# Ten heads instead of eight transposed on TensorE, and their normalisation shared between ScalarE and POOL

## The chip, the cores and the metric

One core of a Trainium2 chip runs one program. The time is device microseconds of one execution; beside it stands a profiled execution of the same kernel. The engines are called PE (TensorE; PEld is its weight load), DVE (VectorE), ACT (ScalarE), POOL (GpSimd) and SP (SyncE, which here only starts DMAs).

## What is computed

Attention over four batches of eight heads, 768 positions of 64 columns, in which a query sees only the keys with its own hash bucket (six signs of a random projection); then, for each of the 3072 positions, a two-layer network with a squared ReLU. The weights come as 64-bit floats, so the kernel has to decode them.

```
q_bits = (einsum('bhsd,dk->bhsk', q, proj) > 0)          # 6 bits, the same for k
mask   = q_bucket[:, :, :, None] == k_bucket[:, :, None, :]
scores = scale * matmul(q, k.transpose(0, 1, 3, 2))
scores = where(mask, scores, -1e9);  scores -= max(scores, -1)
attn   = exp(scores);  attn = attn / (sum(attn, -1) + 1e-9)
x      = matmul(attn, v)                                  # then (tokens, 512)
h = x @ w_in;  r = maximum(h, 0.0);  g = s * (r * r) + b
out = g @ w_out
```

## The kernel before

The program is a list of steps (`Plan.add`, `Plan.any`), each with an engine, a cost, what it reads and writes, and a priority (lower goes first). `Plan.order` runs a list scheduler over these numbers once, while the program is built: at each point an engine that is free takes the ready step with the lowest priority. A step with several ways (`any`) goes to the engine on which it would end first. What comes out is a fixed order on every engine, and on the chip each engine works through its order, waiting at each instruction for what it needs. So a change of a cost or a priority moves instructions everywhere behind it.

**Slots.** The attention is cut into 96 slots: 4 batches x 8 heads x 3 groups of 256 queries. A slot has two tiles of 128 queries by 768 keys. Per tile PE computes the masked scores into two PSUM banks (L568, L569; the mask is part of the product), DVE takes the row maximum (L573), ACT the exponential with its row sum (L574). Small steps on POOL (L578, L579) and DVE (L584, L585) form the reciprocal of the sum, and `norm` (L594, on POOL) multiplies the tile by it and adds the value that a row without any key gets.

**Two ways to the second product.** Its left operand is the tile transposed. In the first `FULL` heads (early) PE transposes the f32 tile, 12 transposes a slot in three steps (L621), ACT or DVE copies each step out of PSUM (L199 to `tb`), and PE multiplies it with the values (L628). In the later heads (`late(w)`) ACT writes the f16 high part (L598), DVE the low part (L599), SP starts a DMA transpose of each tile (L600), and PE multiplies with f16 values (L635).

**Before each head** PE transposes its queries and keys (L438) and computes the hash (L455 to L457), DVE makes the mask rows from it (L459), and DMAs copy them into place (`aq<-aq`, `ks<-nat`, `bq<-nat`) before the head's first score. These pieces get the priority `pr + PP` and are placed between the steps of the slots before (`between`, L636).

**Weights.** 32 blocks of 512 KB come in on ACT's DMA queue (L339) and are decoded on ACT, DVE and POOL (L343 to L354 and L356 to L387); `decodes` (L746) asks for 0.8 blocks a slot from the fourth slot on, and for six a slot from slot 21. For w_out the last step is the low part, high part subtracted from the value (L354); for w_in high and low part are scaled (L381, L386) by a power of two that needs the maximum over all partitions, which `spread` gets by a PE transpose of a broadcast column into PSUM (L394).

**The network.** When all eight heads of a batch have a group of 256 positions (xsb, written at L662 to L666 and passed through DRAM), `moe` takes it: eight rounds of a first product (L702 to L704), a chain on ACT and POOL (L712 to L716) and a second product (L727 to L729). Its steps have a priority behind those of the attention and fill PE where that leaves room; batch 0 can start at slot 21, and what is left after slot 95 runs alone.

Of the kernel before, what the change touches and what calls it, by code (L numbers as in the profile page):

```python
# [139 lines left out]
def lsh_attention_moe(ctx: ExitStack, tc, q, k, v, proj, w_in, w_out, s, b, out):  # L140
# [26 lines left out]
    def f32(ap):  # L167
        return ap.bitcast(F32)
# [8 lines left out]
    def pe(cost, fn, r, w, pr):  # L177
        plan.add(PE, cost, fn, r, w, pr)
# [7 lines left out]
    def pool(n, fn, r, w, pr, ns=None):  # L186
        plan.add(POOL, (0.15 + n / 430.0 if ns is None else ns), fn, r, w, pr)
# [135 lines left out]
    def decode(u, pr):  # L323
# [24 lines left out]
        if not wi:  # L348
            def swap():
                wt[key] = wk.tile([P, 2, 512], F32R, tag=f"w{u}", name=f"w{u}")  # L350
            pool(512, lambda: nc.gpsimd.tensor_tensor(gi, gi, raw()[:, :, 0], ALU.add), rk, [gk], pr)
            plan.add(None, 0.0, swap, [], rk + wk_, pr)
            copy(512, lambda: wt[key][:, 0], lambda: g, [gk], [key + (0,)], pr, (ACT, POOL))
            pool(512, lambda: nc.gpsimd.tensor_tensor(wt[key][:, 1], g, f32(wt[key][:, 0]), ALU.subtract), [gk, key + (0,)], [key + (1,)], pr)  # L354
            return
        pool(512, lambda: nc.gpsimd.tensor_tensor(raw()[:, :, 0], gi, raw()[:, :, 0], ALU.add), [gk], rk, pr)  # L356
        held_raw.append((raw, rk, key))
# [15 lines left out]
        for raw_, rk_, key_ in held_raw:  # L373
            def split(raw_=raw_, rk_=rk_, key_=key_):
                def swap():
                    wt[key_] = wk.tile([P, 2, 512], F16, tag=f"wi{key_[1]}_{key_[2]}", name=f"wi{key_[1]}_{key_[2]}")

                def src_():
                    return raw_()[:, :, 0].bitcast(F32)
                plan.add(None, 0.0, swap, [], [key_ + (0,), key_ + (1,)], pr)  # L380
                some(512, lambda e: e.activation(wt[key_][:, 0], src_(), AF.Copy, scale=up) if e is nc.scalar else e.tensor_scalar(wt[key_][:, 0], src_(), up, None, ALU.mult), rk_ + [("wsc", n)], [key_ + (0,)], pr, (ACT, POOL))  # L381

                def rest():
                    nc.gpsimd.tensor_scalar(src_(), src_(), up, None, ALU.mult)
                    nc.gpsimd.tensor_tensor(wt[key_][:, 1], src_(), wt[key_][:, 0], ALU.subtract)
                plan.any([(DVE, 0.75, lambda: nc.vector.scalar_tensor_tensor(wt[key_][:, 1], src_(), up, wt[key_][:, 0], ALU.mult, ALU.subtract)),  # L386
                          (POOL, 1.95, rest)], [("wsc", n), key_ + (0,)], rk_ + [key_ + (1,)], pr)  # L387
            split()
        held_raw.clear()

    def spread(m, mk_, pr):


        pe(0.12, lambda: nc.tensor.transpose(out=bank[:, 4, CH:CH + P], in_=m.broadcast_to([P, P]), identity=ident), [mk_], ["all"], pr)  # L394
        return bank[:, 4, CH:CH + P], "all"

    def inverse_power(up, down):

# [154 lines left out]
    def weights(i, pr):  # L553

        bb, h, c, w = slots[i]
        x, y = w % 2, i % NST
        aq, bq, ks = AQ[x], BQ[x], KS[x]
        nm, z, rz, u, big_ = [st[:, y, m] for m in range(5)]
        nk, zk = [[("st", y, m, a) for a in range(TPC)] for m in range(2)]
        for a in range(TPC):  # L560
            t, j = c * TPC + a, TPC * i + a
            b0 = (6 if i < EARLY else TWO if late(w) else 0) if j % 2 else 0
            bk = [("b", b0), ("b", b0 + 1)]
            ts = slice(t * P, (t + 1) * P)
            for g in range(2):
                def mm(g=g, ts=ts, b0=b0):
                    cols, o = slice(g * HS, (g + 1) * HS), bank[:, b0 + g, 0:HS]
                    nc.tensor.matmul(o, aq[:, ts], ks[0][:, cols], start=True, stop=False)  # L568
                    nc.tensor.matmul(o, bq[0:HR, ts], ks[1][0:HR, cols], start=False, stop=True)  # L569
                pe(mmc(HS, 2), mm, AK(x) + KK(x) + BK(x), [bk[g]], pr)  # L570
            e, ek = EB[ering(j)], EK[ering(j)]
            sc = bank[:, b0:b0 + 2, 0:HS]
            dve(S, lambda a=a, sc=sc: nc.vector.tensor_reduce(nm[:, a:a + 1], sc, AX.XY, ALU.max, negate=True), bk, [nk[a]], pr, 0.95)  # L573
            act(S, lambda a=a, sc=sc, e=e: nc.scalar.activation(e.rearrange("p (g n) -> p g n", g=2), sc, AF.Exp, bias=nm[:, a:a + 1], accum_out=z[:, a:a + 1]),  # L574
                bk + [nk[a]], [ek, zk[a]], pr, 0.28)

        def missing():
            nc.gpsimd.tensor_scalar(big_, nm, -FLOOR, 1e30, ALU.is_gt, ALU.mult)  # L578
            nc.gpsimd.tensor_scalar(u, nm, -FLOOR, 1.0 / (S + EPS), ALU.is_gt, ALU.mult)  # L579
        pool(TPC, missing, nk, [("st", y, 3), ("st", y, 4)], pr, 0.5)  # L580

        def inverse():
            for a in range(TPC):
                nc.vector.tensor_scalar(rz[:, a:a + 1], z[:, a:a + 1], EPS, big_[:, a:a + 1], ALU.add, ALU.add)  # L584
            nc.vector.reciprocal(rz, rz)  # L585
        dve(1, inverse, zk + [("st", y, 4)], [("st", y, 2)], pr, 0.5)
        for a in range(TPC):
            j = TPC * i + a
            e, ek = EB[ering(j)], EK[ering(j)]
            n, r = j % 2, i % 2  # L590
            hi, lo, hk = pb[:, n, 0], pb[:, n, 1], EK[NE + n]

            def norm(eng, a=a, e=e):
                eng.tensor_scalar(e, e, rz[:, a:a + 1], u[:, a:a + 1], ALU.mult, ALU.add)  # L594
            pool(S, lambda norm=norm: norm(nc.gpsimd), [("st", y, 2), ("st", y, 3)], [ek], pr, NORM if late(w) else 1.02)
            if not late(w):
                continue
            act(S, lambda e=e, hi=hi: nc.scalar.mul(hi, e, TOP), [ek], [hk], pr)  # L598
            dve(S, lambda e=e, hi=hi, lo=lo: nc.vector.scalar_tensor_tensor(lo, e, TOP, hi, ALU.mult, ALU.subtract), [ek, hk], [("lo", n)], pr, 1.0)  # L599
            plan.add(SP, TCOST, lambda a=a, n=n, r=r: nc.sync.dma_start_transpose(tb[:, r, a].rearrange("p h t q -> p (h t) q"), pb[:, n].rearrange("p h n -> p (h n)")),  # L600
                     [hk, ("lo", n)], TK(r, a, 2), pr, TLAG)
# [4 lines left out]
    def values(i, pr, pieces):  # L606
# [48 lines left out]
        if hh:  # L655
# [7 lines left out]
                pool(CH, lambda: nc.gpsimd.tensor_tensor(xsb[:, 1, :], t, xsb[:, 0, :], ALU.subtract), xk + [("xs", 0)], [("xs", 1)], pr)  # L663
            else:
                some(CH, lambda e: e.activation(xsb[:, 0, :], t, AF.Copy, scale=up) if e is nc.scalar else e.tensor_scalar(xsb[:, 0, :], t, up, None, ALU.mult), xk + [("sc", bb)], [("xs", 0)], pr, (ACT, POOL))
                dve(CH, lambda: nc.vector.scalar_tensor_tensor(xsb[:, 1, :], t, up, xsb[:, 0, :], ALU.mult, ALU.subtract), xk + [("sc", bb), ("xs", 0)], [("xs", 1)], pr, 0.45)  # L666
            xd[key] = tc.dram_tile([P, 2, CH], F16, name=f"xd{key[0]}_{key[1]}_{key[2]}")
            plan.add(SP, 0.7, lambda: nc.sync.dma_start(xd[key], xsb), [("xs", 0), ("xs", 1)], [("xd", key)], pr, 131072 / RATE_DMA)

# [135 lines left out]
QDUP = "pool"  # L805
RATE_DMA = 2.2e5
GATE = lambda KK, AK: AK(0)
FULL = 8
FPC = 0.62
WP = -8  # L810
MP = 0.0
PP = -5


# [24 lines left out]
```

## Time and profile before

| | us |
|---|---|
| median of 3 runs (range) | 1024.14 (1021.83 to 1026.34) |
| the profiled execution, and its span in the profile | 1022.31, 1020.5 |
| PE busy | 935.1 (92%) |
| DVE, ACT, POOL busy | 654.9 (64%), 644.9 (63%), 636.2 (62%) |

The span is what the instructions cover; the 1.8 us beside it lie before and after them. The profiled execution is 1.8 us below the median. A busy share is an average over stages that differ: the first 24 slots with nothing but attention and decoding, the stretch in which the network begins, a long middle with both, and the end with the network alone. Waits are put down to what released them last.

### The profile page before, as it was taken

The page shows a single profiled execution, that of the slowest core. Times are in us where ns is not written, and L with a number is a line of the kernel's source. Part 1 is how long each engine was busy: PE and PEld are TensorE (multiplying, and loading weights), DVE is VectorE, ACT ScalarE, POOL GpSimd, SP SyncE. Part 2 cuts the span into 40 slices and gives each one's busy share as a digit, 9 for nine tenths or more (in the row PEclk, how much of TensorE's full clock was granted, in tenths as well). Part 3 has the DMA queues.
Part 4 walks back from the last instruction along what each step waited for, and adds up shares of the span by engine and source line. Part 5 has one row for each costly group of instructions (what it writes and reads, how often), then busy time and mean ns, then how long its engine had stood idle before and what let it go on. Part 6 is the DMA issues. An engine that isn't in the chain of part 4 may idle for free.

```text
span 1020.5 us, 17422 instructions
## 1 busy us (share of the span) xinstructions
PE 935.1 (92%) x6080; PEld 742.6 (73%) x6080; DVE 654.9 (64%) x1189; ACT 644.9 (63%) x1165; POOL 636.2 (62%) x707
## 2 busy tenths in 40 slices
PE   6879787788489999999999999999999999999998
PEld 5656455566267887777888887787888888888886
DVE  6878788789687887877887777876678841000000
ACT  3667677776477676677767776776776764434442
POOL 2455756879497766766667776767766864333333
PEclk7999789889699999999999999999999999999999
DMA  3376475567949897898798989989798862101000
GB/s 100 103 197 182 103 193 145 161 190 154 176 94 179 159 195 169 165 194 186 164 188 187 174 174 195 168 168 200 146 181 187 153 129 63 42 1 42 12 22 21
DMA packets 319080, 144.41 MB, mean 142 GB/s; under 512 B 282688, under 2 KB 303680, under 8 KB 318992
## 3 DMA queue, kind: packets, MB, share of 16 engines
q1 hardware_dynamic: 313792, 126.25, 59.5%
q10 hardware_dynamic: 5200, 17.05, 5.8%
q8 instruction: 48, 0.79, 0.3%
q14 instruction: 40, 0.33, 0.1%
HBM read 48.24 MB, written 12.58 MB: 60 GB/s over the span
## 4 chain that ended last, share of the span: by engine, by line
PE 39%; issue 12%; POOL 10%; DVE 5%; DMA 3%; ACT 2%; SPq 0%; POOLq 0%; DVEq 0%; ACTq 0%
PE bank L635 7%; POOL glb L716 4%; PE bank L729 4%; PE bank L727 4%; PE bank L728 4%; PE bank L702 4%; PE bank L568 4%; PE bank L704 4%; PE bank L703 4%; PE bank L569 3%; POOL rb L715 3%; DVE pb L599 2%; DMA tb<-pb 2%; DVE st L573 1%; PE bank L438 1%
## 5 line engine op out<-in xcount | busy, mean ns | idle before, releaser
L594 POOL TENSOR_SCALAR eb<-eb,st 128x768 f32<-128x768 f32 x179 | 213.4, 1197 | 69.9 <-DVE st L585 66.7
L702 PE MATMUL bank<-xc,wi 128*128 128x256 f16 x768 | 211.7, 276 | 5.9 <-POOL wi L381 2.6
L573 DVE TENSOR_REDUCE st<-bank 128x1 f32<-128x768 f32 x192 | 181.1, 953 | 56.1 <-PE bank L569 45.2
L703 PE MATMUL bank<-xc,wi 128*128 128x256 f16 x768 | 209.8, 273 | 1.4 <-DVE wi L386 1.4
L704 PE MATMUL bank<-xc,wi 128*128 128x256 f16 x768 | 209.9, 273 | 0.0
L574 ACT ACTIVATE eb<-bank,st 128x768 f32<-128x768 f32 x179 | 160.2, 895 | 65.3 <-DVE st L573 53.9
L599 DVE SCALAR_TENSOR_TENSOR pb<-eb,pb 128x768 f16<-128x768 f32 x144 | 161.4, 1124 | 48.0 <-ACT pb L598 47.4
L568 PE MATMUL bank<-ks,aq 128*128 128x384 f32 x384 | 151.1, 393 | 26.1 <-ACT eb L574 14.1
L715 POOL TENSOR_SCALAR rb<-rb,misc 128x512 f32<-128x512 f32 x96 | 84.5, 881 | 141.2 <-ACT ghb L714 140.8
L727 PE MATMUL bank<-w,ghb 128*128 128x512 f32 x384 | 160.4, 418 | 0.0
L729 PE MATMUL bank<-w,glb 128*128 128x512 f32 x384 | 153.5, 400 | 7.4 <-POOL glb L716 7.2
L728 PE MATMUL bank<-w,ghb 128*128 128x512 f32 x384 | 151.9, 396 | 0.4 <-POOL w L354 0.4
L598 ACT ACTIVATE pb<-eb 128x768 f16<-128x768 f32 x144 | 120.1, 836 | 36.7 <-DMA tb<-pb 26.8
L569 PE MATMUL bank<-ks,bq 76*128 76x384 f32 x384 | 135.5, 353 | 5.6 <-DMA bq<-nat 3.7
L716 POOL TENSOR_TENSOR glb<-rb,ghb 128x512 fp32r<-128x512 f32 x96 | 131.1, 1366 | 5.5
L712 ACT ACTIVATE rb<-bank,dsc 128x512 f32<-128x512 f32 x74 | 50.9, 688 | 125.5 <-PE bank L704 115.9
L635 PE MATMUL bank<-tb,vb 128*128 128x256 f16 x864 | 108.2, 276 | 12.4 <-DMA tb<-pb 11.7
L568 PEld LDWEIGHTS bank<-ks,aq 128*128 128x128 f32 x384 | 76.2, 198 | 49.4 <-ACT eb L574 20.7
L702 PEld LDWEIGHTS <-wi 128*128 128x128 f16 x768 | 75.1, 98 | 44.3 <-issue 34.6
L740 DVE COPY osb<-bank 128x256 f32<-128x256 f32 x4 | 1.5, 420 | 163.3 <-PE bank L729 162.7
L635 PEld LDWEIGHTS <-vb 128*128 128x128 f16 x864 | 81.5, 99 | 34.0 <-issue 23.1
L578 POOL TENSOR_SCALAR st<-st 128x2 f32<-128x2 f32 x96 | 40.4, 421 | 90.7 <-DVE st L573 81.7
(128 smaller groups left out, 1656.9 us busy)
## 6 DMA issues: line engine op xcount, KB each, us to landing
ks<-aq SPq DMA_DIRECT2D x60, 192.0 KB
raw<-in_moe_w_in_dram ACTq DMA_DIRECT2D x16, 512.0 KB
raw<-in_moe_w_out_dram ACTq DMA_DIRECT2D x16, 512.0 KB
nat<-in_q_dram SPq DMA_DIRECT2D x32, 192.0 KB
nat<-in_k_dram SPq DMA_DIRECT2D x32, 192.0 KB
vm<-in_v_dram SPq DMA_DIRECT2D x32, 192.0 KB
xd<-xsb SPq DMA_DIRECT2D x48, 128.0 KB
xc<-xd SPq DMA_DIRECT2D x48, 128.0 KB
```

Source lines behind the costliest of these rows:

```text
L568: nc.tensor.matmul(o, aq[:, ts], ks[0][:, cols], start=True, stop=False)
L573: dve(S, lambda a=a, sc=sc: nc.vector.tensor_reduce(nm[:, a:a + 1], sc, AX.XY, ALU.max, negate=True), bk, [nk[a]], pr, 0.95)
L594: eng.tensor_scalar(e, e, rz[:, a:a + 1], u[:, a:a + 1], ALU.mult, ALU.add)
L599: dve(S, lambda e=e, hi=hi, lo=lo: nc.vector.scalar_tensor_tensor(lo, e, TOP, hi, ALU.mult, ALU.subtract), [ek, hk], [("lo", n)], pr, 1.0)
L635: nc.tensor.matmul(av, VB[x][:, kt].rearrange("p z d -> p (z d)"), t[:, :, h, kt], start=(h == kt == 0), stop=(h == 1 and kt == NT - 1))
L702: nc.tensor.matmul(hp, w[:, 0, fs], xc[:, 0, :], start=(cc == 0), stop=False)
L703: nc.tensor.matmul(hp, w[:, 1, fs], xc[:, 0, :], start=False, stop=False)
L704: nc.tensor.matmul(hp, w[:, 0, fs], xc[:, 1, :], start=False, stop=(cc == NC_ - 1))
L716: pool(2 * CH, lambda r=r, gh=gh, gl=gl: nc.gpsimd.tensor_tensor(gl, r, f32(gh), ALU.subtract), [rk, hk], [lk], MP)
L727: nc.tensor.matmul(o, gh[:, ts], w[:, 0], start=(f == 0), stop=False)
L728: nc.tensor.matmul(o, gh[:, ts], w[:, 1], start=False, stop=False)
L729: nc.tensor.matmul(o, gl[:, ts], w[:, 0], start=False, stop=(f == NF - 1))
```

## The change

Five things are edited; the line numbers of the changed program are up to nine higher.

- `FULL` goes from 8 to 10: the heads 8 and 9, the slots 24 to 29, take the early way, with transposes on PE.
- The normalisation of an early tile may go to POOL (cost `NORM`, 1.1, where it was 1.02) or to ACT (0.87), as the scheduler finds.
- In decoding, the low part of a w_out block may go to DVE (0.85) besides POOL (1.4); the cost of w_in's low part on DVE is 0.9 where it was 0.75. The low part of an early result (xsb) may go to POOL as two instructions (1.3) besides DVE (0.6, was 0.45).
- `spread` writes into unused columns of bank 0, one of the score banks, where it wrote into those of bank 4, the bank of the second product.
- `PP` goes from -5 to 0: the pieces that prepare the next heads get a later priority.

```
-            pool(512, lambda: nc.gpsimd.tensor_tensor(wt[key][:, 1], g, f32(wt[key][:, 0]), ALU.subtract), [gk, key + (0,)], [key + (1,)], pr)
+            plan.any([(POOL, 1.4, lambda: nc.gpsimd.tensor_tensor(wt[key][:, 1], g, f32(wt[key][:, 0]), ALU.subtract)),
+                      (DVE, 0.85, lambda: nc.vector.tensor_tensor(wt[key][:, 1], g, f32(wt[key][:, 0]), ALU.subtract))], [gk, key + (0,)], [key + (1,)], pr)
...
-                plan.any([(DVE, 0.75, lambda: nc.vector.scalar_tensor_tensor(wt[key_][:, 1], src_(), up, wt[key_][:, 0], ALU.mult, ALU.subtract)),
+                plan.any([(DVE, 0.9, lambda: nc.vector.scalar_tensor_tensor(wt[key_][:, 1], src_(), up, wt[key_][:, 0], ALU.mult, ALU.subtract)),
...
-        pe(0.12, lambda: nc.tensor.transpose(out=bank[:, 4, CH:CH + P], in_=m.broadcast_to([P, P]), identity=ident), [mk_], ["all"], pr)
-        return bank[:, 4, CH:CH + P], "all"
+        pe(0.12, lambda: nc.tensor.transpose(out=bank[:, 0, HS:HS + P], in_=m.broadcast_to([P, P]), identity=ident), [mk_], ["all"], pr)
+        return bank[:, 0, HS:HS + P], "all"
...
-            pool(S, lambda norm=norm: norm(nc.gpsimd), [("st", y, 2), ("st", y, 3)], [ek], pr, NORM if late(w) else 1.02)
+            ways = [(POOL, NORM, lambda norm=norm: norm(nc.gpsimd))]
+            if not late(w):
+                ways.append((ACT, 0.87, lambda a=a, e=e: nc.scalar.activation(e, e, AF.Identity, bias=u[:, a:a + 1], scale=rz[:, a:a + 1])))
+            plan.any(ways, [("st", y, 2), ("st", y, 3)], [ek], pr)
...
-                dve(CH, lambda: nc.vector.scalar_tensor_tensor(xsb[:, 1, :], t, up, xsb[:, 0, :], ALU.mult, ALU.subtract), xk + [("sc", bb), ("xs", 0)], [("xs", 1)], pr, 0.45)
+
+                def rest():
+                    nc.gpsimd.tensor_scalar(t, t, up, None, ALU.mult)
+                    nc.gpsimd.tensor_tensor(xsb[:, 1, :], t, xsb[:, 0, :], ALU.subtract)
+                plan.any([(DVE, 0.6, lambda: nc.vector.scalar_tensor_tensor(xsb[:, 1, :], t, up, xsb[:, 0, :], ALU.mult, ALU.subtract)), (POOL, 1.3, rest)],
+                         [("sc", bb), ("xs", 0)], xk + [("xs", 1)], pr)
...
-FULL = 8
+FULL = 10
...
-PP = -5
+PP = 0
```

Of the 60 normalisations of the ten early heads ACT gets 35 and POOL 25; of the 44 of the first 22 slots, 24 and 20. Of the 16 low parts of w_out DVE gets 10 and POOL 6; three low parts of w_in and three of xsb go to POOL as two instructions each. The order on ACT near the start, from the third exponential on, before:

```order
L574 ACTIVATE eb,st<-bank,st 128x768 x3
L539 ACTIVATE vm,vmx<-vm 128x384
L574 ACTIVATE eb,st<-bank,st 128x768
L199 COPY tb<-bank 128x512
L574 ACTIVATE eb,st<-bank,st 128x768
L653 ACTIVATE xpb<-bank 64x256
L199 COPY tb<-bank 128x512
L574 ACTIVATE pb,st<-bank,st 128x768
L539 ACTIVATE vm,vmx<-vm 128x384
```

And of the changed program at the same place (L575 is now the exponential, L598 the normalisation, L657 the result's copy):

```order
L575 ACTIVATE eb,st<-bank,st 128x768 x3
L598 ACTIVATE eb<-eb,st 128x768
L575 ACTIVATE eb,st<-bank,st 128x768
L199 COPY tb<-bank 128x512 x2
L575 ACTIVATE eb,st<-bank,st 128x768
L598 ACTIVATE eb<-eb,st 128x768
L657 ACTIVATE xpb<-bank 64x256
L575 ACTIVATE pb,st<-bank,st 128x768
L199 COPY tb<-bank 128x512 x2
L598 ACTIVATE eb<-eb,st 128x768
```

About every second exponential is now followed by a normalisation, which waits for a reciprocal of DVE, and the next exponential stands behind it.

The order on SP while the heads 8 and 9 are computed, before (L600 is the DMA transpose of a tile, L175 and L415 are copies and loads for the next heads, L527 loads values):

```order
L600 DMA_TRANSPOSE tb<-pb 128x12x128 x2
L175 DMA ks_70<-aq_66 64x768
L600 DMA_TRANSPOSE tb<-pb 128x12x128
L175 DMA ks_70<-aq_66 64x768
L175 DMA ks_70<-bq_68 64x768
L600 DMA_TRANSPOSE tb<-pb 128x12x128
L175 DMA aq_66<-aq_66 64x768
L175 DMA ks_70<-nat_65 12x768
L175 DMA bq_68<-nat_65 12x768
L600 DMA_TRANSPOSE tb<-pb 128x12x128 x2
```

And of the changed program (L538 loads values for their maximum, L697 loads the network's input):

```order
L175 DMA ks_70<-aq_66 64x768 x2
L538 DMA vm<-in_v_dram 128x384
L175 DMA ks_70<-bq_68 64x768
L528 DMA vn<-in_v_dram 128x384
L538 DMA vm<-in_v_dram 128x384 x2
L175 DMA aq_66<-aq_66 64x768
L697 DMA xc_1_1_2465<-xd_2_1_147 128x512
L697 DMA xc_1_1_2465<-xd_3_1_150 128x512
L175 DMA ks_70<-nat_65 12x768
L175 DMA bq_68<-nat_65 12x768
```

No transpose stands here any more; the first comes with head 10, some 20 rows further on. On ACT's queue the last weight block is asked for at the exponentials of slot 29 before and of slot 28 now, so before the first transposes of head 10.

On PE, from the last hash product of head 2 to its first score (`ks_70`), before:

```order
L457 MATMUL bank<-bq_68,pj_118 64x384
L628 MATMUL bank<-tb,vb_80 64x256 x6
L568 MATMUL bank<-ks_71,aq_67 128x384
L569 MATMUL bank<-ks_71,bq_69 128x384
L568 MATMUL bank<-ks_71,aq_67 128x384
L569 MATMUL bank<-ks_71,bq_69 128x384
L621 MATMUL bank<-ident,eb 128x128 x12
L568 MATMUL bank<-ks_70,aq_66 128x384
```

And of the changed program, where four more scores of head 1 and four transposes stand between the hash and these rows (L632 is the second product, L625 the transpose):

```order
L632 MATMUL bank<-tb,vb_80 64x256 x6
L395 MATMUL bank<-ident,vmx 128x128
L569 MATMUL bank<-ks_71,aq_67 128x384
L570 MATMUL bank<-ks_71,bq_69 128x384
L569 MATMUL bank<-ks_71,aq_67 128x384
L570 MATMUL bank<-ks_71,bq_69 128x384
L625 MATMUL bank<-ident,eb 128x128 x12
L632 MATMUL bank<-tb,vb_80 64x256 x6
L569 MATMUL bank<-ks_70,aq_66 128x384
```

More of PE's work now stands between this hash and the score that needs it.

## Rows read from the trace of the kernel before

**Rows 1.** Stages: start:end length, busy us (instructions) per engine, clock, DMA share, GB/s

```profile
12.00:174.50 162.50, 130.97 (x770) 91.95 (x770) 131.59 (x281) 109.14 (x232) 88.05 (x112) 0.89 0.55 145
174.50:330.00 155.50, 122.80 (x732) 91.98 (x731) 124.45 (x229) 103.28 (x190) 121.09 (x112) 0.89 0.71 160
330.00:830.00 500.00, 487.93 (x3317) 400.74 (x3316) 382.38 (x632) 350.94 (x626) 351.31 (x402) 1.00 0.87 174
830.00:1020.50 190.50, 185.39 (x1231) 151.82 (x1228) 8.71 (x16) 78.82 (x115) 73.10 (x73) 1.00 0.14 38
```

**Rows 2.** The same view around the first late heads

```profile
214.00:256.80 42.80, 36.14 (x200) 27.57 (x199) 37.70 (x66) 28.33 (x50) 37.36 (x31) 0.92 0.70 159
256.80:277.60 20.80, 6.78 (x24) 4.49 (x24) 12.16 (x27) 8.73 (x15) 10.73 (x10) 0.58 1.03 173
277.60:330.00 52.40, 46.60 (x303) 36.70 (x304) 42.54 (x73) 37.48 (x70) 41.19 (x41) 0.97 0.65 137
```

**Rows 3.** PE in order of time there: start, us, what, [idle before, releaser]

```profile
265.81 2.72 PE L635 MATMUL bank<-tb,vb 128*128 128x256 f16 x12 [9.05 <-DMA tb<-pb]
```

**Rows 4.** SP's queue in order of time there

```profile
260.62 8.54 SPq L600 DMA_TRANSPOSE tb<-pb  x2
```

**Rows 5.** PE in order of time: transposes and second products of a slot

```profile
26.46 2.31 PE L621 MATMUL bank<-ident,eb 128*128 128x128 f32 x12
30.96 1.47 PE L621 MATMUL bank<-ident,eb 128*128 128x128 f32 x12
52.97 1.51 PE L628 MATMUL bank<-tb,vb 128*64 128x256 f32 x12
819.70 1.48 PE L635 MATMUL bank<-tb,vb 128*128 128x256 f16 x12
```

**Rows 6.** Windows again, a stretch full of transposes

```profile
30.00:35.00 5.00, 5.00 (x40) 3.55 (x37) 3.87 (x9) 2.81 (x7) 1.32 (x4) 1.00 0.18 51
```

**Rows 7.** Groups by line: count | busy us, mean ns | idle before, releaser

```profile
L594 POOL TENSOR_SCALAR eb<-eb,st 128x768 f32<-128x768 f32 x179 | 213.4, 1197 | 69.9 <-DVE st L585 66.7 <-PE bank L457 1.5 <-ACT xpb L653 0.5
L599 DVE SCALAR_TENSOR_TENSOR pb<-eb,pb 128x768 f16<-128x768 f32 x144 | 161.4, 1124 | 48.0 <-ACT pb L598 47.4 <-issue 0.3
L598 ACT ACTIVATE pb<-eb 128x768 f16<-128x768 f32 x144 | 120.1, 836 | 36.7 <-DMA tb<-pb 26.8 <-POOL eb L594 6.5 <-DVE st L573 2.1
L714 ACT ACTIVATE ghb<-rb,misc 128x512 fp32r<-128x512 f32 x96 | 77.8, 811 | 1.7
L713 ACT ACTIVATE rb<-rb 128x512 f32<-128x512 f32 x96 | 60.4, 629 | 9.2 <-DVE rb L712 7.6
L199 ACT COPY tb<-bank 128x512 f32<-128x512 f32 x49 | 27.7, 585 | 26.6 <-PE bank L621 21.9 <-issue 4.7
L354 POOL TENSOR_TENSOR w<-osb,w 128x512 fp32r<-128x512 f32 x16 | 22.3, 1395 | 2.9 <-ACT w L199 2.9
L199 DVE COPY tb<-bank 128x512 f32<-128x512 f32 x23 | 15.4, 685 | 2.6 <-PE bank L621 2.5
```

**Rows 8.** What PE waited for, 0 to 174 us: total, times, longest

```profile
PE bank L568 <- ACT eb L574: 6.6, 4, 3.6
PE bank L621 <- POOL eb L594: 6.0, 5, 2.8
PE bank L568 <- DMA aq<-aq: 4.3, 3, 2.4
PE bank L569 <- DMA bq<-nat: 3.5, 2, 2.4
```

**Rows 9.** What POOL waited for, 12 to 174 us

```profile
POOL eb L594 <- DVE st L585: 19.9, 10, 4.0
```

**Rows 10.** PE from the last hash product of head 4 to its first score

```profile
85.50 0.34 PE L457 MATMUL bank<-bq,pj 128*64 128x384 f32 x1
85.68 0.34 PE L568 MATMUL bank<-ks,aq 128*128 128x384 f32 x1
...
91.87 0.44 PE L568 MATMUL bank<-ks,aq 128*128 128x384 f32 x1 [0.17 <-DMA vm<-in_v_dram]
```

## The prediction

> **What bounds the kernel now.** I read the stages first, in the view of busy time by windows [rows 1]. From 330 us to the end PE is busy 487.9 of 500 and 185.4 of 190.5 us: there PE's own work is the time, and what any other engine does is hidden as long as it keeps up (DVE, the next, has 382 of 500). Before 330 us PE is not the bound. From 12 to 174.5 us, the slots 0 to 21 with no network work yet, PE has 131 of 162.5, DVE 131.6, ACT 109 and POOL 88. From 174.5 to 330 us PE has 122.8 of 155.5, DVE 124.5, POOL 121. PE is idle for 31.5 and 32.7 us there, against 17.2 in the 690 us after. So the end moves with three things: how long the first stage takes until the network can start, how long the second takes until PE is full, and how much PE work there is in all.
>
> Next I cut the second stage around its worst place [rows 2]. From 256.8 to 277.6 us PE is busy 6.8 of 20.8 us, at a mean granted clock of 0.58, and every other engine is at half of its time or a little over: nothing is short but the DMA engines, whose share is 1.03. In order of time PE stands 9.05 us before a second product of a late head, on the DMA transpose of its probabilities [rows 3], and SP needs 8.54 us to start two transposes [rows 4] where weight blocks load on ACT's queue. Behind that product in PE's order stand the scores of two tiles and the broadcast for the scale of the last w_in blocks, so decoding and the network wait too.
>
> **The change part by part.**
>
> *Heads 8 and 9 by PE transposes.* PE's price: a slot's 12 transposes take 1.47 us and its second product 1.51, where the f16 product took 1.48 [rows 5]. That is 1.50 us a slot more, 9.0 us for six slots. ACT loses 12 x 836 = 10.0 us of high parts, DVE 12 x 1124 = 13.5 us of low parts; 18 copies come back, of which the order gives about nine to DVE (9 x 685 = 6.2) and nine to ACT (9 x 585 = 5.3) [rows 7]. SP and the DMA engines lose 12 transposes, and the first one now comes after the last weight block was asked for. So the stall of rows 2 has no cause left where it stood. Its whole worth is 14.0 us of PE idle, plus about 3 us because 6.8 us of work ran near half clock: 17 us.
>
> How much of that can be had? The other engines' work of that stretch stays. From 214 to 330 us DVE has 92.4 us in 116 [rows 2]. It loses 13.5, gains 6.2 of copies and some eight low parts of w_out; DVE does not do that operation before, so between zero and 8 x 1395 (POOL's own time [rows 7]); the nearest DVE row with two inputs is the low part of a tile, 1124 for 768 columns, 749 in proportion to 512; I take 0.9 us, between these two, so 7.2. The sum is 92.3. The fullest that DVE gets here is 37.7 of 42.8 us, 88%. At that share the stretch needs 105 us, 11 less than now. PE: 89.5 + 9.0 - 3 = 95.5 us, at the 89% of 277.6 to 330 us 107 us, 9 less. POOL falls by about 11 normalisations of 1.2 and eight low parts of 1.4, 24 of its 89, and drops out. I take **-10 us** for this stretch, with PE's 9.0 us already inside; ends: -17 - 3 if DVE can be fuller and POOL's relief helps, and 0 if it only reorders.
>
> *Normalisation on ACT.* ACT does no such instruction before. Two instructions of 512 columns bound it: 629 without and 811 with two operands read per row, a difference of 182 [rows 7]; added to the 836 of 768 columns that is 1.02 us, not the 0.87 of the plan; below it cannot be 0.84, above POOL's 1.20 is far enough. In the first stage 24 of 44 go there: ACT 109 + 24.5 = 134 us of 162.5, about DVE's share; POOL loses some 27 us that it did not lack. What it can give is latency: a pair of normalisations ran one after the other on POOL, and PE waited 6.0 us for it before transposes [rows 8]. I take -2. What it can cost: behind a normalisation on ACT the next exponential is queued, and for that PE waits already (6.6 us); I take +1.5. Ends: -6 and +12 (rival C).
>
> *PP and the new places of the preparing pieces.* From the last hash product of a head to its first score at least 6 us pass for the mask and three DMAs: 85.50 + 0.34 to 91.87 [rows 10]. PE waited 4.3 + 3.5 us on these DMAs [rows 8]. Counting PE's rows between the two places for the heads 2 to 7 in both orders, at 0.18 us a product of 384 columns (85.50 to 85.68), 0.12 a transpose and 0.25 a second-product row (a twelfth and a sixth of [rows 5]), gives 28 us of cover before and 32 now (head 2: 3.7 and 6.5; head 5 has 3.4 in both). I take **-2**, between 0 and -4.
>
> *The rest.* Spread in a score bank: eight broadcasts that now share their bank with scores and exponentials; at the longest such wait, 3.6 us [rows 8], at most 8 x 3.6, but each has the same kind of neighbour in bank 4 before; 0 taken. Three low parts of w_in and three of xsb on POOL: two instructions of at most 1.4 each, 17 us on an engine that has lost over 50; hidden, and 0 to +2 if one stands before a first network product. The changed costs alone do nothing. After 330 us the order is shuffled over 17 us of idle: 0, +-3.
>
> *A rule against it.* PE ran twelve transposes in 2.31 us at one time and in 1.47 at another [rows 5], and the second fell into a window with the full clock, 2.4 GHz, throughout [rows 6]. The Trainium skill, "TensorE: Matmul & The Clock Gate", Part 4, says that transposes do not count as PE being busy in the same way and that the full clock does not engage for them. By that rule six slots with 72 more of them would lose clock (rival D); this trace does not bear it out in that window.
>
> **Sum.** -10 + (-2 + 1.5) - 2 = -12.5 us. The profiled execution took 1022.3 us, so 1009.8; the median lies 1.8 us above it, so **1011.6 us**, about 1.2% less.
>
> **Rivals.** What this kernel can tell from no change is about 0.5%, 5 us.
>
> A, larger: the second stage gains all of its 17 us and DVE's relief from POOL, -20, and the first -6 by parallel normalisations: 1024 - 26 = 998. For it: POOL's load falls everywhere. Against: DVE at 88% nowhere got fuller.
>
> B, slower: the stall belongs to the change-over, not to its place. If the first transposes of head 10 stand as long at slot 30, then the 14 us come back where PE would be full, with PE's 9.0 us paid: -2.5 + 9.0 = +6.5, 1030.6. For it: the first transposes share SP's queue with the copies for the next heads there too. Against: before, the first two late products waited little and the third met the weight loads; those are asked for earlier now. It decides from about 12 of the 14 us on.
>
> C, ACT the bound of the first stage: POOL waited 19.9 us for DVE's reciprocals [rows 9], on an engine that had nothing else; if ACT inherits that wait with the instructions, its 134 us become 153, which at 88% takes 174 us, 12 more than now. Then -10 - 2 + 12 = 0: 1024. Against: the order mostly puts an exponential before each of them, which gives DVE the time.
>
> D, transposes at low clock: 6 x (2.31 - 1.47) = 5.0 us, 1016.6.
>
> E, PE pays and no more: DVE's share stays at its 80% of that stretch, only half of the stall comes back: -8.5 + 9.0 x 0.5 = -4, and -2.5: 1017.6 to 1020.
>
> **How the numbers follow.** Forecast 0.46, A 0.11, B 0.12, C 0.13, D 0.05, E 0.13. The forecast's own range is 1003 to 1019. Faster by over 0.5% (under 1019.0): the forecast, A, most of D, two thirds of E and a little of C, 0.68. Slower (over 1029.3): B, and C with a bad second stage, 0.13. The same: 0.19. The range 999 to 1028 leaves out the far part of A and most of B.
>
> **What would show it.** Right: no PE wait on a DMA transpose of 5 us or more between the slots 24 and 32; the stretch from the first network product (174.5 us now) to the point where PE is full shorter by about 10 us; PE busy about 6 us more in all; the first network product at 172 us, give or take 5. B is shown by such a wait near head 10; C by waits of PE or DVE for exponentials in the first stage well over 6.6 us and a first network product after 182 us; D by a granted clock below 0.9 over the slots 24 to 29 without idle. Wrong as a whole: PE idle before 330 us no less than 64 us.

## The result, and the profile after

The changed kernel took 1006.56 us in the median of four runs (1005.77 to 1007.07), the kernel before on the same chip 1024.96. The ratio is **0.9836, with an interval of 0.9802 to 0.9871**: 1.6% faster, where 1.2% was forecast. The profiled execution took 1006.61 us, its span is 1004.8.

The stages after, in the view of busy time by windows, cut at the first network product (now 167.45 us) and at 330 and 830 us; columns as in [rows 1]:

```profile
12.00:167.45 155.45, 127.58 (x766) 91.51 (x766) 131.47 (x282) 123.72 (x241) 67.93 (x94) 0.90 0.54 146
167.45:330.00 162.55, 145.48 (x891) 106.15 (x889) 133.16 (x251) 116.66 (x210) 110.80 (x111) 0.94 0.54 141
330.00:830.00 500.00, 492.53 (x3345) 407.84 (x3345) 385.24 (x630) 350.61 (x628) 351.13 (x396) 0.99 0.88 175
830.00:1004.80 174.80, 169.97 (x1123) 138.91 (x1121) 4.95 (x8) 70.78 (x103) 64.92 (x65) 1.00 0.10 29
```

The network starts 7.0 us earlier, and what follows its start is 8.7 us shorter, 837.3 for 846.0. In these two profiled executions PE is busy 944.1 us in all, 9.0 more, and idle 24.7 us less. Of these, 19.3 lie between 12 and 330 us (64.2 idle before, 44.9 now) and 4.9 behind (17.2 and 12.3). At 330 us the program is ahead: 662.5 us of PE's work are left, where 673.3 were.

The last two of these windows are those of [rows 2]; the first begins at 174.5 us instead of 214:

```profile
174.50:256.80 82.30, 72.56 (x436) 50.32 (x435) 73.36 (x146) 67.58 (x123) 57.40 (x57) 0.92 0.59 171
256.80:277.60 20.80, 19.17 (x116) 14.16 (x116) 18.53 (x36) 11.72 (x20) 15.99 (x14) 0.92 0.28 75
277.60:330.00 52.40, 50.93 (x321) 39.59 (x322) 37.10 (x67) 34.42 (x62) 31.26 (x36) 0.97 0.58 120
```

The hole is filled: PE runs 116 instructions where it ran 24, and the DMA engines' share is 0.28 where it was 1.03. PE's waits from 174 to 330 us (total, times, longest) no longer name a DMA transpose, against [rows 3]:

```profile
PE bank L625 <- DVE bq L442: 4.2, 1, 4.2
PE bank L625 <- ACT eb L598: 3.3, 4, 1.3
PE bank L712 <- DVE wi L387: 2.2, 3, 1.0
PE bank L632 <- DVE tb L199: 2.1, 3, 1.1
```

SP's queue now has the first transposes at head 10, started in 3.42 us, where [rows 4] has 8.54:

```profile
303.37 3.42 SPq L604 DMA_TRANSPOSE tb<-pb  x2
```

The groups that answer to [rows 7], by line and form (L595 and L598 are the normalisation, L355 the low part of w_out on DVE):

```profile
L595 POOL TENSOR_SCALAR eb<-eb,st 128x768 f32<-128x768 f32 x149 | 183.1, 1234 | 71.4 <-DVE st L586 59.0 <-ACT tb L199 6.0 <-ACT osb L344 3.3
L603 DVE SCALAR_TENSOR_TENSOR pb<-eb,pb 128x768 f16<-128x768 f32 x132 | 147.7, 1121 | 44.2 <-ACT pb L602 42.9 <-ACT rb L721 0.3
L598 ACT ACTIVATE eb<-eb,st 128x768 f32<-128x768 f32 x27 | 27.1, 1021 | 7.5 <-DVE st L586 6.9 <-DVE vmx L542 0.4
L355 DVE TENSOR_TENSOR w<-osb,w 128x512 fp32r<-128x512 f32 x10 | 7.7, 769 | 0.7 <-ACT w L199 0.6
```

The ACT normalisation takes 1021 ns, where 1.02 us had been put together from two shorter rows. The low part on DVE takes 769 ns (0.9 assumed).

PE's waits in the first stage, 0 to 167.45 us, against [rows 8]: the five longest in total, then the other waits for normalisations.

```profile
PE bank L439 <- DMA nat<-in_k_dram: 4.7, 2, 3.4
PE bank L569 <- ACT eb L575: 4.5, 2, 3.6
PE bank L625 <- POOL eb L595: 4.3, 4, 2.8
PE bank L625 <- DVE bq L442: 3.4, 3, 1.7
PE bank L632 <- DVE tb L199: 2.5, 1, 2.5
PE bank L625 <- POOL pb L595: 1.2, 1, 1.2
PE bank L625 <- ACT pb L598: 1.0, 1, 1.0
PE bank L625 <- ACT eb L598: 0.6, 1, 0.6
```

Before, one more wait for a normalisation stands beside those of [rows 8]:

```profile
PE bank L621 <- POOL pb L594: 0.6, 1, 0.6
```

What POOL waited for before its normalisations from 12 to 167.45 us, against [rows 9]:

```profile
POOL eb L595 <- DVE st L586: 7.1, 3, 3.1
```

And what ACT waited for before its own, in the same stretch:

```profile
ACT eb L598 <- DVE st L586: 1.9, 5, 0.5
```

The waits on the mask's DMAs fell from 7.8 to 0.8 us. Those on normalisations did not get shorter in sum: 6.6 us before, 7.1 now (5.5 for POOL's, 1.6 for ACT's). Longer ones on the preparation of keys (`bq`, `nat`) stand beside them: the list changed more than its sum. One wait of 4.2 us on `bq` follows the first network product; it is the one in the list from 174 us on.

### The profile page after: what moved, and what is told of

Read it like the earlier page. It is cut to its first block, busy times and chain, and to the rows that moved or that the text cites. A ratio compares the mean times of both kernels' runs of the same rounds, so it can differ in the third digit from the quotient of the medians.

```text
span 1004.8 us, 17499 instructions
## 1 busy us (share of the span) xinstructions
PE 944.1 (94%) x6152; PEld 750.7 (75%) x6152; DVE 662.2 (66%) x1202; ACT 664.4 (66%) x1182; POOL 597.4 (59%) x674
## 4 chain that ended last, share of the span: by engine, by line
PE 58%; issue 12%; POOL 11%; DVE 10%; DMA 5%; ACT 2%; SPq 0%; POOLq 0%; DVEq 0%; ACTq 0%
PE bank L639 8%; PE bank L569 6%; PE bank L570 5%; PE bank L711 5%; PE bank L738 5%; PE bank L736 5%; PE bank L737 5%; PE bank L712 5%; PE bank L713 5%; POOL glb L725 4%; DMA tb<-pb 3%; PE bank L625 3%; PE bank L632 3%; DVE st L574 2%; POOL rb L724 2%
## 5 line engine op out<-in xcount | busy, mean ns | idle before, releaser
L595 POOL TENSOR_SCALAR eb<-eb,st 128x768 f32<-128x768 f32 x149 | 183.1, 1234 | 71.4 <-DVE st L586 59.0
L575 ACT ACTIVATE eb<-bank,st 128x768 f32<-128x768 f32 x176 | 157.6, 896 | 57.0 <-DVE st L574 45.4
L603 DVE SCALAR_TENSOR_TENSOR pb<-eb,pb 128x768 f16<-128x768 f32 x132 | 147.7, 1121 | 44.2 <-ACT pb L602 42.9
L724 POOL TENSOR_SCALAR rb<-rb,misc 128x512 f32<-128x512 f32 x96 | 81.9, 853 | 144.3 <-ACT ghb L723 142.7
L602 ACT ACTIVATE pb<-eb 128x768 f16<-128x768 f32 x132 | 110.2, 837 | 35.6 <-DMA tb<-pb 21.6
L721 ACT ACTIVATE rb<-bank,dsc 128x512 f32<-128x512 f32 x70 | 48.2, 688 | 129.2 <-PE bank L713 121.6
L639 PE MATMUL bank<-tb,vb 128*128 128x256 f16 x792 | 98.9, 275 | 2.9 <-DMA tb<-pb 2.8
L639 PEld LDWEIGHTS <-vb 128*128 128x128 f16 x792 | 74.9, 98 | 22.0 <-issue 9.3
```

Of the source, the lines that this page charges most:

```text
L639: nc.tensor.matmul(av, VB[x][:, kt].rearrange("p z d -> p (z d)"), t[:, :, h, kt], start=(h == kt == 0), stop=(h == 1 and kt == NT - 1))
```

## The experiments

Ratios are to the kernel before, run on the same chip in the same session. "First" is PE's first network product, "idle" PE's idle time from 12 to 330 us, the last three columns are PE's busy time, its clock and the DMA share in the window from 240 to 285 us. Every column but the ratio comes from one profiled execution. Before and e9 have the same order, so their two rows show by how much one order's profiles differ.

| run | ratio (interval) | first | idle | PE in 45 us | clock | DMA |
|---|---|---|---|---|---|---|
| before | 1 | 174.5 | 64.2 | 26.6 | 0.77 | 0.87 |
| after | 0.9836 (0.9802 to 0.9871) | 167.5 | 44.9 | 39.9 | 0.92 | 0.39 |
| e1 ten heads | 0.9923 (0.9897 to 0.9948) | 172.7 | 45.8 | 37.7 | 0.96 | 0.41 |
| e2 normalisation | 0.9927 (0.9899 to 0.9955) | 168.6 | 56.9 | 31.1 | 0.85 | 0.74 |
| e3 after, eight heads | 0.9896 (0.9859 to 0.9932) | 171.2 | 52.8 | 31.7 | 0.81 | 0.60 |
| e4 after, norm on POOL | 0.9887 (0.9842 to 0.9933) | 178.4 | 47.2 | 40.8 | 1.00 | 0.41 |
| e5 both, nothing else | 0.9843 (0.9791 to 0.9895) | 171.4 | 39.9 | 42.9 | 1.00 | 0.48 |
| e6 after, PP -5 | 0.9849 (0.9808 to 0.9891) | 171.1 | 44.7 | 39.2 | 1.00 | 0.45 |
| e7 two costs up | 0.9871 (0.9827 to 0.9915) | 166.5 | 58.6 | 30.0 | 0.92 | 0.61 |
| e8 loads earlier | 0.9880 (0.9835 to 0.9926) | 199.8 | 56.4 | 41.9 | 1.00 | 0.72 |
| e9 bank alone | 0.9985 (0.9951 to 1.0018) | 175.4 | 58.5 | 27.9 | 0.81 | 0.83 |
| e10 one cost, 0.02 | 0.9928 (0.9892 to 0.9963) | 179.9 | 57.3 | 31.8 | 0.85 | 0.78 |
| e11 two costs down | 0.9873 (0.9816 to 0.9931) | 166.9 | 55.9 | 34.2 | 0.85 | 0.67 |
| e12 after, one cost, 0.02 | 0.9843 (0.9790 to 0.9895) | 166.7 | 47.9 | 42.9 | 1.00 | 0.52 |

All kernels made from before carry the broadcast of `spread` in bank 0, as the change has it.

### e1 and e2: one half of the change each

```
-FULL = 8
+FULL = 10
```

> The kernel before with two edits: ten heads transposed on PE (FULL 10), and the broadcast of spread in bank 0, which the new order needs. Normalisation stays on POOL, PP and all costs stay. Theory (the second stage gains because the DMA transposes no longer meet the weight loads): the 9.05 us wait on a DMA transpose is gone, PE is idle some 10 us or more less between its first network product (174.5 us in the kernel before) and full PE, PE busy +9 us, first network product unchanged at 173 to 176 us, total 1014 to 1018 us, ratio about 0.991. Rival R (any neutral edit reshuffles the order and moves the time by several us; the ten heads as such give nothing): total within 5 us of the kernel before, or slower by up to the 9 us that PE pays (1025 to 1034), with long waits of another kind in the second stage. Rival N (the gain is the normalisation's): the stall is replaced by waits on POOL for normalisations before the transposes of heads 8 and 9, total 1020 or more.

Measured 0.9923, 1014.8 us, a total as the theory had it. The long wait is gone and idle falls by 18 us. PE now waits more for normalisations that POOL alone makes (L621; 7.5 us before). Its two longest waits in total, 12 to 330 us:

```profile
PE bank L621 <- POOL eb L594: 11.4, 10, 2.8
PE bank L568 <- ACT eb L574: 8.6, 10, 3.7
```

e2 leaves eight heads and adds the choice:

```
-pool(S, lambda norm=norm: norm(nc.gpsimd), ..., NORM if late(w) else 1.02)
+ways = [(POOL, NORM, ...)]
+if not late(w):
+    ways.append((ACT, 0.87, ...))
+plan.any(ways, ...)
```

> The kernel before with two edits: the normalisation of an early tile goes to POOL or ACT as the scheduler finds, and the broadcast of spread in bank 0. Eight heads stay on PE, PP stays -5. Theory (the first stage's gain of 7 us is the two engines' normalising at the same time): first network product at 168 to 171 us instead of 174.5, PE's waits for a normalisation before its transposes in the first stage shorter than the 6.0 us of before, the 9 us wait on a DMA transpose in the second stage still there, total 1016 to 1020 us. Rival P (the first stage's gain comes from the later place of the preparing pieces, PP 0): first network product at 173 to 176 us, total within 5 us of the kernel before. Rival C (ACT becomes the bound): first network product after 178 us.

Measured 0.9927, 1013.7 us, more than expected. The first product came at 168.6 us as forecast, but the wait on a DMA transpose did not stay: the longest is 1.5 us, with eight heads still. Other waits stand in the window instead, and PE is busy 31.1 of its 45 us.

### e3 and e4: the change without one half

e3 is the changed kernel with `FULL = 8`; e4 has the old `pool(...)` call with 1.02.

> The changed kernel with eight heads transposed on PE instead of ten; all else of the change stays. Theory: a PE wait on a DMA transpose of 5 us or more comes back near slots 24 to 27, PE busy falls by about 9 us but idle rises by 15 or more, first network product stays near 167.5 us, total 1013 to 1018 us. Rival M (the other edits of the change already move weight loads and POOL's work so that no stall would be left): no such wait, total 998 to 1003 us, faster than the changed kernel by the 9 us that PE no longer pays. Rival R (reshuffling): total anywhere in 1005 to 1025 with no wait on a DMA transpose above 3 us.

> The changed kernel with the normalisation of early tiles on POOL alone at the cost of before (1.02); ten heads, PP 0 and the other edits stay. Theory (first stage gained by the parallel normalisation): first network product at 171 to 175 us instead of 167.5, PE's waits on POOL before transposes back to 6 us or more, and more such waits in the slots 24 to 29, where POOL now has all of them; total 1011 to 1016 us. Rival P (PP gave the first stage): first network product stays at 167 to 169 us, total within 3 us of the changed kernel's 1006.6.

e3: 0.9896, 1011.3 us. The total is below the theory's range, and no wait on a DMA transpose came back; nor did the time fall by PE's 9 us; rival R, a total anywhere with no such wait, is what came. The window is hollow again (31.7 of 45 us), with waits on POOL's part of the network (`glb`, 9.7 us from 12 to 330 us). e4: 0.9887, 1010.9 us, first product at 178.4 (171 to 175 expected), and PE waits for POOL's normalisations 14.8 + 3.1 us (12 to 330 us; 4.3 + 1.2 in the changed kernel):

```profile
PE bank L622 <- POOL eb L595: 14.8, 13, 2.1
PE bank L622 <- POOL pb L595: 3.1, 5, 1.1
```

By these ratios each half is worth 5 to 6 us when the other is there, and about 8 alone; how much of that is only a new order can't be read from them. The stall's disappearance in e2 and e3 says that it hung on the order, which every edit changes. The next runs test that.

### e5 and e6: both halves, and PP

e5 joins e1 and e2. e6 is the changed kernel with `PP = -5`.

> The kernel before with ten heads transposed on PE, the normalisation of early tiles on POOL or ACT, and the broadcast of spread in bank 0; PP stays -5 and the new costs and ways of decoding are left out. Alone the first edit gave a ratio of 0.9923 (about -8 us) and the second 0.9927 (about -7.5). Theory (the two gains lie in two stages and add up, the rest of the change is worth nothing): ratio 0.983 to 0.986, total 1005 to 1009 us, first network product at 167 to 171 us, PE idle before 330 us 42 to 48 us. Rival S (they share one gain, either edit breaks up the bad place and the second adds only PE's 9 us): ratio 0.990 to 0.995. Rival P (the remaining edits carry part of it): ratio 0.987 to 0.990.

> The changed kernel with PP back at -5 (the pieces that prepare a head as early as before). Theory (PP gives the cover between hash and first score, -2 us by the prediction): PE waits again for the mask's DMAs before scores, 5 us or more in the first stage (0.8 in the changed kernel), and less for the transposes that the later pieces delay; total 1007 to 1011 us. Rival Q (the later pieces cost what they give: PE's 7.6 us of waits on the copies of the keys' transposes before the next head's, which were not there before, go as the mask's waits come): total within 2 us of 1006.6. Rival R (the order shifts by chance): 1000 to 1004 or over 1012 with no such pattern in the waits.

e5: 0.9843, 1003.5 us; e6: 0.9849, 1006.2 us. Neither can be told from the changed kernel. The new decoding ways and PP together, and PP alone, are worth nothing that these runs can measure. The total of e6 is rival Q's, but not its mechanism. With the old PP the mask's DMAs (`aq`, `bq<-nat`) cost PE only 1.7 us of waits from 12 to 170 us, and the keys' preparation (`nat`, `bq`) 7.9; the changed kernel has 0.8 and 8.1 there. The 7.6 us in the expectation include the 4.2 that lie behind the first network product.

### e7: a control that moves two costs

```
-plan.any([(DVE, 0.75, ...
+plan.any([(DVE, 0.9, ...
...
-..., [("xs", 1)], pr, 0.45)
+..., [("xs", 1)], pr, 0.6)
```

> A control for the scheduler's reshuffling: the kernel before with the broadcast of spread in bank 0, and only two cost numbers raised as in the change (the low part of w_in on DVE 0.75 to 0.9, of the result 0.45 to 0.6). No instruction changes its engine for a reason of its own; only the order moves. Theory (a reshuffle alone is worth little): first network product at 174.5 us, the wait on a DMA transpose near slot 24 still several us, total within 3 us of before. Rival R (any edit that moves the order past the place of the stall breaks it up): the 9 us wait gone or under 3 us, total 1012 to 1018 us, as much as either real edit gave alone.

Measured **0.9871, 1006.9 us**: more than either half, against the theory. The windows up to the first product, to 330 us, and on:

```profile
12.00:166.54 154.54, 124.81 (x750) 88.39 (x748) 131.21 (x276) 108.42 (x230) 86.26 (x111) 0.91 0.54 152
166.54:330.00 163.46, 134.60 (x822) 102.27 (x821) 132.50 (x240) 112.62 (x205) 136.25 (x128) 0.93 0.68 162
330.00:830.00 500.00, 492.30 (x3354) 406.98 (x3353) 384.77 (x626) 350.77 (x626) 362.01 (x403) 1.00 0.88 175
```

The network starts 8 us earlier with ACT at 108 us, so without any help from it, and in the first two windows PE runs 1572 instructions, where it ran 1502 in those of [rows 1]. The hole is not filled (30.0 of 45 us); it has other names. PE's two longest waits from 240 to 285 us:

```profile
PE bank L394 <- DVE wmx L361: 4.3, 1, 4.3
PE bank L568 <- ACT eb L574: 3.7, 1, 3.7
```

And SP's queue in order of time a little earlier:

```profile
230.64 13.54 SPq L600 DMA_TRANSPOSE tb<-pb  x4
```

Four transposes take 13.54 us to start, 3.4 us each where the two of [rows 4] took 4.3 each, and PE's waits name none of them: in this order other work stands between.

### e8: the loads moved away instead of the transposes

```
-FIRST = 0.8
+FIRST = 1.5
```

> The kernel before with the broadcast of spread in bank 0 and with 1.5 weight blocks a slot decoded from the fourth slot on, where it was 0.8 (FIRST 1.5): more than half of the loads and of the decoding fall before the network starts, so that hardly any loads are left when the first late heads are transposed by DMA. Eight heads stay on PE. Theory (loads beside the transposes cause the stall): no wait on a DMA transpose above 3 us, two transposes start in 4.2 us or less on SP's queue, PE idle between the first network product and 330 us below 22 us; but the first stage gets longer by the decoding it takes in, about 12 blocks of some 3 us on the fullest engine, so that the first network product comes after 180 us; total 1010 to 1030 us. Rival T (the stall belongs to the transposes and the change of way as such): a wait of 5 us or more on a DMA transpose at the heads 8 or 9 in spite of few loads.

Measured 0.9880, 1009.4 us. The hole is filled with eight heads and their DMA transposes in it, here from 240 us on in steps of ten:

```profile
240.00:250.00 10.00, 8.93 (x57) 7.02 (x56) 8.65 (x15) 7.66 (x17) 9.75 (x10) 1.00 0.54 124
250.00:260.00 10.00, 9.96 (x73) 8.15 (x70) 8.57 (x14) 7.34 (x14) 9.83 (x10) 1.00 0.87 172
260.00:270.00 10.00, 8.22 (x50) 6.55 (x51) 8.09 (x14) 5.80 (x12) 9.83 (x9) 1.00 0.60 116
270.00:280.00 10.00, 9.79 (x69) 7.76 (x68) 7.79 (x24) 8.33 (x15) 9.20 (x11) 1.00 0.82 125
```

Two transposes start in 3.3 to 3.6 us there. The first stage pays: the first product comes at 199.8 us. So the hole needs the late heads and the weight blocks at one time; in these orders taking away either fills it. Whether the blocks' loads or their decoding matter more, e8 doesn't part, since it moves both.

### e9 to e11: the bank, and two more reorderings

e9 has the bank alone, in the order of before. e10 adds a move of two hundredths, e11 lowers the costs that e7 raised:

```
-NORM = 1.1
+NORM = 1.12
...
-plan.any([(DVE, 0.75, ...
+plan.any([(DVE, 0.65, ...
-..., [("xs", 1)], pr, 0.45)
+..., [("xs", 1)], pr, 0.35)
```

> The kernel before with one edit, the broadcast of spread in bank 0 instead of bank 4; the order of every engine is that of the kernel before, row for row. All kernels that were faster so far contain this edit. Theory O (order: what the faster kernels share is that their order is another one): no difference, 1018 to 1024 us, ratio 0.997 to 1.003, with the same 9 us wait on a DMA transpose near 265 us. Rival K (the bank: in bank 4 the broadcast holds up second products until its reader is done): most of the gain of 8 to 13 us of the other runs is there with this edit alone, 1008 to 1014 us.

> The kernel before with the broadcast of spread in bank 0 and one cost number moved by two hundredths: the normalisation of a late tile on POOL, 1.12 instead of 1.10 in the plan. No way is added; the orders are the same as before until the first network products (about 175 us) and differ behind them. Theory O (the order of before stands in an unlucky place in the second stage, and nearly any other order avoids it): first network product at 174.5 us as before, no wait of 5 us or more on a DMA transpose, PE idle from there to 330 us 5 to 12 us less than 32.7, total 1010 to 1016 us. Rival U (orders scatter to both sides): total anywhere from 1012 to 1032, so that this run alone can also come out slower. Rival L (the stall has a cause in what work there is, not in its order): the stall stays, 1018 to 1024 us.

> A second control in the other direction: the kernel before with the broadcast of spread in bank 0 and the two costs that e7 raised lowered by a tenth (low part of w_in on DVE 0.75 to 0.65, of the result 0.45 to 0.35); the kernel before has in its trace 0.747 and 0.484 us for these, so both directions lead away from what the instructions take. e7 with the costs raised took 0.9871 of the time of before. Theory O (before is an unlucky order): also faster than before by 5 us or more, 1005 to 1016 us. Rival V (raised costs make the plan better, lowered ones worse): 1020 us or more. Rival U (orders scatter to both sides): anywhere from 1005 to 1035.

e9: 0.9985, no difference: the bank is not it. It keeps the stall, in order of time on PE:

```profile
267.06 2.72 PE L635 MATMUL bank<-tb,vb 128*128 128x256 f16 x12 [7.49 <-DMA tb<-pb]
```

And on SP's queue, where the transposes that it waits for start:

```profile
263.44 6.96 SPq L600 DMA_TRANSPOSE tb<-pb  x2
```

e10: 0.9928, 1012.5 us. Its order leaves before's only at about 215 us (DVE) and 220 us (PE) of before's time, so its gain comes from there on; PE's longest wait on a DMA transpose from 12 to 330 us is 0.8 us. (Its profiled execution took 1019.2 us, 7 above its median, so its other columns in the table say little.) e11: 0.9873, 1009.1 us, the same as e7 with the opposite edit. The 0.747 and 0.484 us in e11's expectation are medians; the means in the kernel before are 0.944 and 0.594, to which e7's numbers lie nearer. But e11 leads away from both and gains as much, so truer costs are not the reason.

Three edits of cost numbers alone, called neutral reorderings here, gave 7 to 13 us, and none lost: the order of before is a poor one. They are not pure reorderings, though. Where a step has several ways, the plan also picks other engines: e7 gives two of the 16 low parts of w_in to POOL, which before has all on DVE, and e10 has 30 of 36 high parts of late results on ACT, where before has 23. The runs don't part the new order from these choices.

### e12: a neutral reordering of the changed kernel

The edit is e10's `NORM`, in the changed kernel.

> The changed kernel with one cost number moved by two hundredths (a normalisation on POOL 1.12 in the plan instead of 1.10): all parts of the change are in, the order is another one from the fourth head on. Three neutral reorderings of the kernel before gave 0.9871, 0.9873 and 0.9928 of its time; the changed kernel and its two kernels with both ten heads on PE and the shared normalisation gave 0.9836, 0.9843 and 0.9849, those with one of the two 0.9887 to 0.9927. Theory B (the two edits together are worth some 4 to 5 us beyond a mere reordering): 0.983 to 0.986, 1004 to 1008 us. Rival W (the two groups are one scatter of orders): anywhere from 0.980 to 0.994, 1002 to 1016 us, and 0.988 or more would speak for it.

Measured 0.9843, 1006.4 us. The four kernels with both halves lie at 0.9836, 0.9843, 0.9843 and 0.9849, the three neutral reorderings of before at 0.9871, 0.9873 and 0.9928, those with one half at 0.9887 to 0.9927. The means of the first two groups, 0.9843 and 0.9891, are 0.5% or 4.9 us apart. All four lie below all the others; the single intervals overlap, so it is likely and not settled that both halves are worth about 5 us beyond a reordering.

Its window from 240 to 285 us, PE's transposes alone in the view by windows (PE and PEld, then clock, DMA share, GB/s):

```profile
240.00:285.00 45.00, 5.62 (x36) 4.08 (x36) 1.00 0.52 151
```

The stretch holds 36 of them, and the granted clock is 1.00 throughout. They are 5.6 of the 42.9 us that PE is busy there, work that a kernel with eight heads on PE does not have in this place.

## Why the prediction was right, and where it was not

- **The total** (1011.6 forecast, 1006.6 measured, -17.5 instead of -12.5 from the 1024.1 it started at) lies in the forecast's own range. The direction was right; the reason given was only a part of it. A term put at nothing moves as much alone as the whole sum of -12.5, so that the total lies in the range is partly luck.
- **The step that failed** is "The changed costs alone do nothing", with "The rest" at 0 to within 3 us. Two costs alone gave -13 (e7, e11), one cost -7 (e10). On top of both halves the new costs give nothing that can be measured (e5), so it is the new plan that gains, not the costs. Among the rivals there was none that any new order gains, though before's order was the only one seen and the stall in it could well be its own. What in that order costs so much is not one wait: e7's first stage is 8 us shorter with 29.7 us of PE idle in it, where before has 31.5. Part of the earlier start is only a new place in PE's order, behind 750 instructions instead of 770. What makes the rest stays open.
- **The stall.** Its place and the meeting of late heads and weight blocks were right: e1 and e8, from two sides, fill the hole and leave no long wait on a transpose. All six kernels with ten heads have 40 to 48 us idle before 330 us, all eight with eight heads 53 to 64. The means, 45.1 and 57.6, are 12.5 apart, of which up to 9.0 is only the work that ten heads give PE. Crediting this edit with the end of the 9.05 us wait was wrong: e2, e3, e7, e10 and e11 lose it in other ways, and most of the hole remains under other names. The stretch was forecast at -10; all that follows the first network product became 8.7 us shorter.
- **PE's price**, 9.0 us, was 9.0 in all in the two profiles compared, but that they agree is luck: before and e9, with the same order, have 935.1 and 942.2 us of PE busy. The eight profiles with eight heads average 938.3, the six with ten 943.4. The 5.1 between them is nearer to the prediction's 6 in all, with 3 us given back by the clock.
- **Normalisation on ACT.** Its price was right, 1.02 us put together and 1021 ns measured. The first stage was put at -2.5 and came out at -7.0, but e7 and e11 have that gain without any of it, and the latency that was to give it did not show: PE's waits for normalisations there were 6.6 us before and 7.1 after. From 12 to 330 us the ten-head kernels without the choice wait 13.0 (e1) and 17.9 us (e4) for POOL's normalisations, those with it 5.5 to 10.3 for either engine's (e5, e6, e12, after). That the choice makes ten heads affordable is likely from this, but not shown: e7 and e8 wait 13.0 and 13.3 us with eight heads and POOL alone, and are faster than e1.
- **PP**, -2: not measurable (e6). The mask waits fell to 0.8 us, but not by PP: they are 1.7 in e6 with the old value, and the waits for the keys' preparation are as long there.
- **Rivals.** B did not come: at head 10 PE's longest wait on a transpose is 1.1 us. C neither: ACT waited 2.6 us for the reciprocals in the first stage (1.9 in the row above and 0.7 before `pb`), not 19.9. D neither: the changed kernel's granted clock is 0.94 from 240 to 300 us, with PE busy 54.6 of 60. It falls to half there, 1.2 GHz, twice (0.50 from 259 to 262 us and from 280 to 282 us), each time behind waits of PE: three between network products, 2.2 us in all, and two before transposes, 1.33 and 0.59 us. And 36 transposes of e12 lie in a stretch with the full clock, 2.4 GHz, throughout. The window of [rows 6] is not full of transposes: they are 12 of its 40 instructions and 1.47 of its 5.00 us. The rule of the Trainium skill, "TensorE: Matmul & The Clock Gate", Part 4, that the full clock does not engage for transposes, is not borne out where they are mixed with products. A was nearest in size, for another reason.

## What to carry to other kernels

Where a scheduler fixes the order, any edit is two edits: what it says, and a new order. Before crediting the first, run controls that move a cost by a few hundredths and change nothing else, several different ones if they can be had; here moves of 0.02 to 0.15 were worth 7 to 13 us, where the whole change gave 17. A long wait in one profile shows where an order is bad, and what can fill the place for good is read from several orders: here each order that filled it had parted the late heads from the weight blocks.

## What was not expected of the hardware

- Starting DMA transposes while weight blocks load can take two to two and a half times as long: 13.54 us for four (e7), 12.47 for three (e11) and 8.54 for two (before), where two take 3.3 to 3.6 us between 257 and 287 us in e8, whose last block was asked for at 229.8. The loads are not all of it: two took 5.65 us at 334 us in e4, long behind its last block (259.4). In e7 and e11 PE's longest wait on a transpose was none and 2.5 us, so the slow start costs much only where PE's product stands close behind.
- One order does not have one first stage: in before, e9 and e10, which share it, the first network product came at 174.5, 175.4 and 179.9 us, at a granted clock of 0.89, 0.86 and 0.84 from 12 us on. Before and e9, whose order is the same to the end, also have 64.2 and 58.5 us of PE idle from 12 to 330 us. So a few us of that stage in a single profile are no evidence, and the -7.0 above is one pair.
